# TensorE's order written out by the program: scores, transposes and weighted values between sixths of a step's feed-forward products

## The chip, the cores and the metric

The kernel runs on one core of a Trainium2 chip. TensorE (PE) multiplies matrices into PSUM; VectorE (DVE), ScalarE (ACT) and GpSimd (POOL) do the work by element; SyncE (SP) issues the DMAs. Each engine takes its instructions in the order in which they stand in its own stream. The metric is the device time of one execution in microseconds (us).

## What is computed

Attention that keeps the 32 largest scores of every row, then a gated feed-forward layer on its output:

```
scores = q @ k.T / 8                     # 8 batches x 8 heads, 576 rows, 64 wide
kth    = 32nd largest score of each row
attn   = softmax over the scores >= kth
x      = attn @ v                        # gathered to 4608 tokens x 512
out    = (sigmoid(x @ w_gate) * (x @ w_val)) @ w_out      # 512 -> 1536 -> 512
```

## The kernel before

**Attention.** A step is one pair of heads `p` (4 pairs), one tile `i` of 128 query rows and one batch: 4 full tiles, and a fifth of 64 rows per head that holds both heads (`i == NT`, half the work). A batch goes in two groups of tiles, (0,1,2) and (3,4) in even batches, (0,1) and (2,3,4) in odd ones; inside a group all tiles of a pair come, then the next pair: 160 steps. A step does the following.

- `begin`/`scores`: TensorE writes a head's scores to `pss` (one PSUM buffer of two banks, pool `ps_s`), ACT copies them to `s` (L228). A full tile has two such blocks, here called block 0 and block 1, for its two heads. The products are of split operands: queries `qh`+`ql` (ACT L190, POOL L191), keys likewise (ACT L171, POOL L173).
- `select`: DVE finds the largest of eight segments (`cand`, L286) and from them three rounds of eight (`tops`, `leads`, L290); ACT marks what lies below (`under`, L298, which waits for `leads`); POOL writes `u` (L304, L305); DVE reads the limit `kths` (L312). ACT makes the exponentials `e` (L235), which wait for a small POOL instruction `st` (L294).
- `masked`: DVE multiplies `e` with the mask (L240); POOL spreads the inverse sum to `inv` (L246).
- `turn`: TensorE transposes `e` in three blocks `pt` (two PSUM buffers), ACT copies each to `et` (L328).
- `weigh`, at a pair's last tile of a group: TensorE makes `po` from `et` and the values (L356, L357), DVE scales it to `xf` (L360), ACT and POOL split it into `xh` and `xl` (L363, L364).

**Feed-forward.** A unit is 384 tokens; there are 12. It has three rounds `g`; a round has four gate/value pairs `pz` of 24 products each (L395 to L397) and then four outputs of 12 products each (L414 to L416), all into `ps_f` (three buffers). After a pair come ACT (tanh, L400), DVE (`gf`, L401), ACT (`gh`, L402) and POOL (`gl`, L403), and the outputs read `gh` and `gl` of all four pairs. The weights come from DRAM, split into a high and a low part; the first pass splits them itself, which takes until the third unit's inputs are first allocated (`split_done`).

**Order.** At iteration `n` the program writes: keys and values of step `n+2`, queries of `n+4`, scores of `n+2`, selection of `n`, mask of `n-1`, then as many feed-forward products as a goal allows that follows the rows already turned (`at`) 480 rows behind, then the transposes of `n-2` and, at a group's end, the weighted values. This is a priority only: a scheduler lays out all instructions on a simulated timeline and puts on each engine what is ready there first. So TensorE's stream is not the order of the program. The weighted values have a raised priority and go from the last tile to the first.

Of the kernel before, what the change touches and what calls it, by code (L numbers as in the profile page):

```python
# [10 lines left out]
F32 = mybir.dt.float32  # L11
# [18 lines left out]
def tile_topk_attention_then_gated_ffn(  # L30
# [30 lines left out]
    FETCH, ASK, AHEAD = 2, 4, 2  # L61
# [132 lines left out]
    def scores(qs, ks, i, nm):  # L194

        J = 2 if i < NT else 1
        s = bs.tile([P, 2, S], F32, tag="s", name=f"s_{nm}")
        K = D if len(qs) == 1 else P
        if K == D and J == 2:
# [9 lines left out]
            return s  # L209
# [21 lines left out]
        return s  # L231
# [83 lines left out]
    def turn(e, inv, i, et, nm):  # L315

        ef = e.rearrange("p j s -> p (j s)")
        if i < NT:
            for g in range(3):
# [8 lines left out]
                nc.scalar.activation(et[:, 3 * g : 3 * g + m], pt[:, :m], AF.Copy)  # L328
        else:
# [3 lines left out]
            for h in range(2):  # L333
                nc.scalar.activation(et[:, 5 * h : 5 * h + 4, :REM], pt[:, :, h * REM : h * REM + REM], AF.Copy)
            pt = ps_t.tile([P, 4, P], F32, tag="t", name=f"pt_{nm}_1")
# [3 lines left out]
            for h in range(2):  # L339
                d = slice(h * D, h * D + D)  # L340
                nc.scalar.activation(et[d, 4:10:5, :REM], pt[d, h : 3 : 2 - h, h * REM : h * REM + REM], AF.Copy)

    def weigh(ets, vt, pieces, nm):
# [7 lines left out]
        with tc.high_priority():  # L351
            lead = None
            for et, c, n in reversed(spans):
                with tc.issue_after(lead.ins) if lead is not None else ExitStack():
                    for a in reversed(range(5)):
                        last = nc.tensor.matmul(po[D:, c], vt[:, 5 + a], et[:, 4 + a, :n], start=a == 4, stop=a == 0)  # L356
                        nc.tensor.matmul(po[:D, c], vt[:, a], et[:, a, :n], start=a == 4, stop=a == 0)  # L357
                lead = last
# [8 lines left out]
    def ffn(nm0, xs, t0, general):  # L367
# [17 lines left out]
        for g in range(NG):  # L385
            gs = []
            for f in range(FG):
# [3 lines left out]
                pz = []  # L391
                for u in range(2):
# [5 lines left out]
                    pz.append(ps)  # L398
                gf = pools["f2"].tile([P, U], F32, tag="gf", name=f"gf_{nm}")
                nc.scalar.activation(gf, pz[0], AF.Tanh, scale=0.5)  # L400
                nc.vector.scalar_tensor_tensor(gf, gf, 1.0, pz[1], op0=ALU.add, op1=ALU.mult)  # L401
# [3 lines left out]
                yield 6 * NP * U  # L405
            for e in range(NE):
                if e % 2 == 0:
                    wt = load(NF + g * (NE // 2) + e // 2)
                nm = f"{nm0}_{g}_{e}"
                if g == 0:  # L410
                    acc[e] = pools["f4"].tile([P, U], F32, tag="acc", name=f"acc_{nm}")
                ps = ps_f.tile([P, U], F32, tag="f", name=f"po2_{nm}")
                for f, (gh, gl) in enumerate(gs):
                    nc.tensor.matmul(ps, wt[:, e % 2, 0, f], gh, start=f == 0, stop=False)  # L414
                    nc.tensor.matmul(ps, wt[:, e % 2, 0, f], gl, start=False, stop=False)  # L415
                    nc.tensor.matmul(ps, wt[:, e % 2, 1, f], gh, start=False, stop=f == FG - 1)  # L416
                if g == 0:
                    nc.scalar.activation(acc[e], ps, AF.Copy, scale=0.5)  # L418
                else:
                    part = pools["f2"].tile([P, U], F32, tag="gf", name=f"part_{nm}")  # L420
# [4 lines left out]
                yield 3 * FG * U  # L425

    def run(general):
# [4 lines left out]
        def fetch(m):  # L432
            if m < len(steps) and steps[m][2] == groups[steps[m][0]][1]:
# [4 lines left out]
                values[g, p] = load_values(b, p, f"{mark}{g}_{p}")  # L438

        def begin(m):  # L440
            if m < len(steps):
                g, p, i = steps[m]
                staged[m] = scores(qs.pop(m), keys[groups[g][0], p], i, f"{mark}{groups[g][0]}_{i}_{p}")
# [6 lines left out]
        for m in range(max(FETCH, ASK)):  # L450
            if m < FETCH:
                fetch(m)
            if m < ASK:
                ask(m)
        for m in range(AHEAD):
            begin(m)
# [138 lines left out]
```

## Time and profile before

| what | value |
|---|---|
| runs (3) | 1634.15, 1638.8, 1639.49 us; median 1638.8 |
| profiled execution | 1635.55 us, span 1633.7 us |
| PE busy | 1551.6 us, 95% of the span |
| DVE, POOL, ACT busy | 1262.6, 1178.9, 1159.4 us (77%, 72%, 71%) |
| DMA | 330 MB, 58% of 16 engines' time on the main queue |

Busy time of PE is the union of its instructions' spans; neighbours overlap, so start-to-start distances tell its pace. "Idle before" names the engine whose semaphore ended a wait.

### The profile page before, as it was taken

Reading aid. Unit: us, or ns where it says so; the run is one execution under the profiler, and the core shown is the slowest. Engines: PE = TensorE matmul, PEld = TensorE weight load, DVE = VectorE, ACT = ScalarE, POOL = GpSimd, SP = SyncE. Lnnn points to the kernel's source line nnn. Section 1 sums busy time; section 2 is a strip of 40 time slices with the busy share of each in tenths; the row PEclk is TensorE's granted clock in tenths of the full one; section 3 lists DMA queues with packets and bytes.
Section 4 is the critical chain, followed back from the end, with each engine's and each line's share of the span. In section 5 each row is a group of like instructions: output and inputs, shape, how many; then the busy total and the mean of one; then the engine's idle time right before and its main releaser. Section 6 shows DMA issues by size and latency. Waiting matters only on the chain. (4 is left out here: it accounts for less than half of the span.)

```text
span 1633.7 us, 35681 instructions
## 1 busy us (share of the span) xinstructions
PE 1551.6 (95%) x11378; PEld 1431.1 (88%) x11378; DVE 1262.6 (77%) x5764; ACT 1159.4 (71%) x2551; POOL 1178.9 (72%) x1907
## 2 busy tenths in 40 slices
PE   5878999999999999999999999989999999999998
PEld 2435797889999899999999999979999989999998
DVE  5999779988788788888788868888878778887400
ACT  6888678878676777778776677777767677776421
POOL 4677878888767787788867786787875797775513
PEclk8878999999999999999999999999999999999999
DMA  8546655755555565556555575555555565554575
GB/s 249 184 163 222 257 174 181 253 196 208 201 202 182 186 235 189 202 192 219 205 208 193 177 251 183 192 194 198 201 198 187 203 221 193 188 195 164 184 270 181
DMA packets 88998, 330.03 MB, mean 202 GB/s; under 512 B 9952, under 2 KB 36576, under 8 KB 61920
## 3 DMA queue, kind: packets, MB, share of 16 engines
q1 hardware_dynamic: 88800, 327.65, 58.0%
q8 instruction: 92, 1.51, 0.4%
q14 instruction: 106, 0.87, 0.2%
HBM read 299.30 MB, written 28.31 MB: 201 GB/s over the span
## 5 line engine op out<-in xcount | busy, mean ns | idle before, releaser
L304 POOL TENSOR_TENSOR u<-s,under 128x288 f32<-128x288 f32 x576 | 423.9, 758 | 116.8 <-ACT under L298 109.8
L286 DVE MAX8 cand<-s 128x8 f32<-128x72 f32 x2304 | 346.3, 217 | 107.5 <-ACT s L228 96.6
L395 PE MATMUL pz<-xh,w 128*128 128x384 f32 x1120 | 382.3, 343 | 1.4 <-ACT xh L363 1.1
L396 PE MATMUL pz<-xl,w 128*128 128x384 f32 x1120 | 380.4, 340 | 2.0 <-POOL xl L364 2.0
L397 PE MATMUL pz<-xh,w 128*128 128x384 f32 x1120 | 380.3, 340 | 0.0
L240 DVE SCALAR_TENSOR_TENSOR e<-s,kths,e 128x576 f32<-128x576 f32 x288 | 289.3, 1010 | 3.2 <-ACT e L235 2.9
L312 DVE MAX8 kths<-u 128x8 f32<-128x584 f32 x288 | 219.4, 762 | 89.1 <-POOL u L305 87.0
L235 ACT ACTIVATE e<-s,st 128x576 f32<-128x576 f32 x288 | 210.2, 773 | 103.9 <-POOL st L294 103.4
L298 ACT ACTIVATE under<-s,leads 128x576 fp8e4<-128x576 f32 x288 | 223.0, 775 | 58.0 <-DVE leads L290 54.7
L403 POOL TENSOR_TENSOR gl<-gf,gh 128x384 fp32r<-128x384 f32 x144 | 151.1, 1050 | 100.2 <-ACT gh L402 97.0
L395 PEld LDWEIGHTS pz<-xh,w 128*128 128x128 f32 x1120 | 210.6, 188 | 3.7 <-ACT xh L363 1.8
L396 PEld LDWEIGHTS pz<-xl,w 128*128 128x128 f32 x1120 | 211.2, 189 | 3.0 <-POOL xl L364 2.9
L397 PEld LDWEIGHTS pz<-xh,w 128*128 128x128 f32 x1120 | 210.9, 188 | 0.3
L328 ACT ACTIVATE et<-pt 128x384 f32<-128x384 f32 (+1 forms) x384 | 193.6, 522 | 22.6 <-PE pt L323 12.3
L323 PE MATMUL pt<-ident,e 128*128 128x128 f32 x1152 | 187.6, 282 | 16.5 <-DVE e L240 13.5
L228 ACT ACTIVATE s<-pss 128x576 f32<-128x576 f32 x256 | 164.8, 644 | 40.5 <-PE pss L221 40.0
L415 PE MATMUL po<-gl,w 128*128 128x384 f32 x560 | 190.0, 340 | 1.0 <-POOL gl L403 1.0
L414 PE MATMUL po<-gh,w 128*128 128x384 f32 x560 | 188.0, 346 | 1.3 <-ACT acc L418 1.2
L416 PE MATMUL po<-gh,w 128*128 128x384 f32 x560 | 188.5, 339 | 0.0
L221 PE MATMUL pss<-k,qh 128*128 128x288 f32 (+2 forms) x588 | 168.5, 304 | 15.2 <-ACT s L228 15.1
L323 PEld LDWEIGHTS pt<-ident,e 128*128 128x128 f32 x1152 | 143.3, 144 | 44.8 <-DVE e L240 12.7
L356 PE MATMUL po<-et,v 128*64 128x128 f32 (+1 forms) x1600 | 178.7, 265 | 0.2 <-ACT et L328 0.2
(97 smaller groups left out, 3344.0 us busy)
## 6 DMA issues: line engine op xcount, KB each, us to landing
w<-ws SPq DMA_DIRECT2D x210, 1024.0 KB, 4.9
v<-in_v_dram SPq DMA_DIRECT2D x64, 320.0 KB, 3.1
wraw<-in_w_dram SPq DMA_DIRECT2D x36, 512.0 KB, 4.4
ws<-wsplit SPq DMA_DIRECT2D x36, 512.0 KB, 3.6
qraw<-in_q_dram SPq DMA_DIRECT2D x140, 128.0 KB, 2.3
kraw<-in_k_dram SPq DMA_DIRECT2D x56, 288.0 KB, 3.2
out_dram<-acc SPq DMA_DIRECT2D x48, 192.0 KB, 3.5
q<-in_q_dram SPq DMA_DIRECT2D x20, 128.0 KB, 3.3
```

What stands on the lines that cost most here:

```text
L235: nc.scalar.activation(e[:, j], s[:, j], AF.Exp, bias=st[:, j : j + 1], scale=1.0 / SHRINK)
L240: nc.vector.scalar_tensor_tensor(e[:, j], s[:, j], kth[j], e[:, j], op0=ALU.is_ge, op1=ALU.mult, accum_out=st[:, 4 + j : 5 + j])
L286: nc.vector.max(cand[:, j, 8 * g : 8 * g + 8], s[:, j, g * SEG : (g + 1) * SEG])
L298: nc.scalar.activation(under[:, j], s[:, j], AF.Sign, bias=bound, scale=-CUT, accum_out=sums[:, j : j + 1], saturate=False)
L304: nc.gpsimd.tensor_tensor(u[:, j, c], s[:, j, c], under[:, j, c], op=ALU.mult)
L312: nc.vector.max(kths[:, at[j] : at[j] + 8], u[:, j])
L323: nc.tensor.transpose(pt[:, c], ef[:, k0 : k0 + P], ident)
L328: nc.scalar.activation(et[:, 3 * g : 3 * g + m], pt[:, :m], AF.Copy)
L395: nc.tensor.matmul(ps, wt[:, u, 0, d], xh, start=d == 0, stop=False)
L396: nc.tensor.matmul(ps, wt[:, u, 0, d], xl, start=False, stop=False)
L397: nc.tensor.matmul(ps, wt[:, u, 1, d], xh, start=False, stop=d == NP - 1)
L415: nc.tensor.matmul(ps, wt[:, e % 2, 0, f], gl, start=False, stop=False)
```

## The change

From the iteration in which the weights are split and the third unit's inputs exist, TensorE's stream is put under a manual schedule: its instructions stand as the program writes them, and the scheduler orders the other engines alone. The step is cut up for that. `scores` and `turn` give up control after each block; `ffn` does so after every three products; `weigh` goes forward, without raised priority, one iteration later (`n-3`). In each iteration six pieces are written, each followed by a sixth of the step's feed-forward products: score block 0, transposes, weighted values, transposes, score block 1, transposes. In a round's outputs the first two outputs take the fourth pair's `gh`/`gl` last. The tanh of a pair is written before the value products. Keys are fetched 4 steps ahead instead of 2, values in the step itself instead of 2 ahead. Before the region starts, the scheduler still orders TensorE.

```diff
-    FETCH, ASK, AHEAD = 2, 4, 2
+    KEYS, ASK, AHEAD = 4, 4, 2
...
     def weigh(ets, vt, pieces, nm):
...
-        with tc.high_priority():
-            lead = None
-            for et, c, n in reversed(spans):
-                with tc.issue_after(lead.ins) if lead is not None else ExitStack():
-                    for a in reversed(range(5)):
...
+        for et, c, n in spans:
+            for a in range(5):
...
                     for d, (xh, xl) in enumerate(xs):
                         nc.tensor.matmul(ps, wt[:, u, 0, d], xh, start=d == 0, stop=False)
                         nc.tensor.matmul(ps, wt[:, u, 0, d], xl, start=False, stop=False)
                         nc.tensor.matmul(ps, wt[:, u, 1, d], xh, start=False, stop=d == NP - 1)
+                        if d < NP - 1:
+                            yield 3 * U
+                    if u == 0:
+                        nc.scalar.activation(gf, ps, AF.Tanh, scale=0.5)
+                        yield 3 * U
...
+            for e0 in range(0, NE, 2):
+                wt = load(NF + g * (NE // 2) + e0 // 2)
+                late = FG - 1 if e0 == 0 else FG
+                for e in (e0, e0 + 1):
+                    outs[e] = ps_f.tile([P, U], F32, tag="f", name=f"po2_{nm0}_{g}_{e}")
+                    for f in range(late):
+                        products(e, f)
+                        if f < FG - 1:
+                            yield 3 * U
+                    if late == FG:
+                        collect(e)
+                        yield 3 * U
+                if late < FG:
+                    for e in (e0, e0 + 1):
+                        products(e, late)
+                        collect(e)
+                        yield 3 * U
...
+        for n in range(len(steps) + 3):
+            if not general and region is None and len(bxs) == 2:
+                region = tc.manual_schedule(engines={mybir.EngineType.PE})
+                region.__enter__()
...
+            fetch_values(n)
+            fetch_keys(n + KEYS)
+            ask(n + ASK)
+            goal = max(at - BEHIND, min((at - U) * 1.5, U)) * per_row
+            first, second = begin(n + AHEAD), turned(n - 2) if 2 <= n < len(steps) + 2 else iter(())
+            if region is None:
...
+            else:
+                choose(n)
+                chunks = [first, second, None, second, first, second]
+                begun = work
+                for t, chunk in enumerate(chunks):
+                    if chunk is not None:
+                        next(chunk, None)
+                    elif 3 <= n:
+                        weighed(n - 3)
+                    more(begun + (goal - begun) * (t + 1) / len(chunks))
```

`choose` is the selection of `n` and the mask of `n-1`; `turned` calls `turn`; `weighed` calls `weigh` and appends finished units.

**First place: a score block and its successor.** On TensorE before, in the sixth batch, pair 1: the second block of tile 2, then the first block of tile 3 (`pss` tile_pair_block).

```order
L221 MATMUL pss_2_1_1_15808<-k_1_3_14449,qh_2_1_15486 128x288
L221 MATMUL pss_2_1_1_15808<-k_1_3_14449,ql_2_1_15487 128x288
L221 MATMUL pss_2_1_1_15808<-k_1_3_14449,qh_2_1_15486 128x288
L221 MATMUL pss_2_1_1_15808<-k_1_3_14449,ql_2_1_15487 128x288
L323 MATMUL pt_2_0_1_16078<-ident,e_2_0_15659 128x128 x3
L323 MATMUL pt_2_0_2_16083<-ident,e_2_0_15659 128x128 x3
L326 MATMUL pt_2_0_2_16083<-ident,inv_2_0_15863 128x128
L221 MATMUL pss_3_1_0_15955<-k_1_2_14443,qh_3_1_15638 128x288
L221 MATMUL pss_3_1_0_15955<-k_1_2_14443,ql_3_1_15639 128x288
L221 MATMUL pss_3_1_0_15955<-k_1_2_14443,qh_3_1_15638 128x288
L221 MATMUL pss_3_1_0_15955<-k_1_2_14443,ql_3_1_15639 128x288
```

On TensorE after the change, at the same place, from the end of the six products that follow the second block of tile 2 to the start of tile 3's first block.

```order
L410 MATMUL po_6_2_1_15877<-gh_2_3_15756,w_16_15865 128x384
L411 MATMUL po_6_2_1_15877<-gl_2_3_15757,w_16_15865 128x384
L412 MATMUL po_6_2_1_15877<-gh_2_3_15756,w_16_15865 128x384
L323 MATMUL pt_1_3_2_15912<-ident,e_1_3_15485 128x128 x3
L326 MATMUL pt_1_3_2_15912<-ident,inv_1_3_15675 128x128
L410 MATMUL po_6_2_2_15920<-gh_2_0_15439,w_17_15918 128x384
L411 MATMUL po_6_2_2_15920<-gl_2_0_15440,w_17_15918 128x384
L412 MATMUL po_6_2_2_15920<-gh_2_0_15439,w_17_15918 128x384
L410 MATMUL po_6_2_2_15920<-gh_2_1_15556,w_17_15918 128x384
L411 MATMUL po_6_2_2_15920<-gl_2_1_15557,w_17_15918 128x384
L412 MATMUL po_6_2_2_15920<-gh_2_1_15556,w_17_15918 128x384
L221 MATMUL pss_3_1_0_15968<-k_1_2_14149,qh_3_1_15622 128x288
```

Where seven transposes stood alone between the two blocks, twelve products and four transposes stand.

**Second place: the last `gl` of a round.** On TensorE before, in unit 5's first round, up to the first product that reads the fourth pair's low part `gl_0_3` (the last gate/value product stands 29 products, 10 transposes and 8 score products ahead of it).

```order
L416 MATMUL po_5_0_2_12773<-gh_0_0_12156,w_13_12770 128x384
L414 MATMUL po_5_0_2_12773<-gh_0_1_12319,w_13_12770 128x384
L415 MATMUL po_5_0_2_12773<-gl_0_1_12320,w_13_12770 128x384
L416 MATMUL po_5_0_2_12773<-gh_0_1_12319,w_13_12770 128x384
L414 MATMUL po_5_0_2_12773<-gh_0_2_12441,w_13_12770 128x384
L415 MATMUL po_5_0_2_12773<-gl_0_2_12442,w_13_12770 128x384
L416 MATMUL po_5_0_2_12773<-gh_0_2_12441,w_13_12770 128x384
L221 MATMUL pss_1_2_0_12254<-k_2_4_12036,qh_1_2_11913 128x288
L221 MATMUL pss_1_2_0_12254<-k_2_4_12036,ql_1_2_11914 128x288
L221 MATMUL pss_1_2_0_12254<-k_2_4_12036,qh_1_2_11913 128x288
L221 MATMUL pss_1_2_0_12254<-k_2_4_12036,ql_1_2_11914 128x288
L415 MATMUL po_5_0_0_12613<-gl_0_3_12477,w_12_12610 128x384
```

On TensorE after the change, the same product of the same unit and round.

```order
L410 MATMUL po_5_0_1_12622<-gh_0_1_12290,w_12_12610 128x384
L411 MATMUL po_5_0_1_12622<-gl_0_1_12291,w_12_12610 128x384
L412 MATMUL po_5_0_1_12622<-gh_0_1_12290,w_12_12610 128x384
L410 MATMUL po_5_0_1_12622<-gh_0_2_12383,w_12_12610 128x384
L411 MATMUL po_5_0_1_12622<-gl_0_2_12384,w_12_12610 128x384
L412 MATMUL po_5_0_1_12622<-gh_0_2_12383,w_12_12610 128x384
L221 MATMUL pss_0_3_1_12637<-k_3_7_12205,qh_0_3_12211 128x288
L221 MATMUL pss_0_3_1_12637<-k_3_7_12205,ql_0_3_12212 128x288
L221 MATMUL pss_0_3_1_12637<-k_3_7_12205,qh_0_3_12211 128x288
L221 MATMUL pss_0_3_1_12637<-k_3_7_12205,ql_0_3_12212 128x288
L410 MATMUL po_5_0_0_12612<-gh_0_3_12495,w_12_12610 128x384
L411 MATMUL po_5_0_0_12612<-gl_0_3_12496,w_12_12610 128x384
```

The third output has moved behind the reading of `gl_0_3`; the last gate/value product stands 19 products, 6 transposes and 4 score products ahead of it.

## Rows read from the trace of the kernel before

**Rows 1.** The page's busy times: engine, us, share, instructions.
```profile
PE 1551.6 (95%) x11378; PEld 1431.1 (88%) x11378; DVE 1262.6 (77%) x5764; ACT 1159.4 (71%) x2551; POOL 1178.9 (72%) x1907
```

**Rows 2.** Busy time by stretch: us, length, each engine, clock, DMA share, GB/s.
```profile
100.00:200.00 100.00, 84.93 (x543) 59.94 (x543) 91.33 (x385) 77.07 (x159) 79.18 (x124) 0.90 0.66 235
...
290.00:1530.00 1240.00, 1215.37 (x9390) 1167.92 (x9389) 1005.86 (x4697) 907.62 (x2032) 943.07 (x1544) 0.99 0.58 200
```

**Rows 3.** Waits from 290 to 1530 us: who for whom, total, times, longest.
```profile
ACT e L235 <- POOL st L294: 100.2, 70, 5.0
...
ACT under L298 <- DVE leads L290: 48.5, 52, 4.8
...
PE pss L221 <- ACT s L228: 15.1, 11, 3.2
```

**Rows 4.** TensorE from 1072 us on: start, us, instruction [idle before <-who].
```profile
1072.90 0.30 PE L221 MATMUL pss<-k,ql 128*128 128x288 f32 x1
1073.03 0.82 PE L323 MATMUL pt<-ident,e 128*128 128x128 f32 x6
1074.32 0.33 PE L326 MATMUL pt<-ident,inv 128*128 128x128 f32 x1 [0.47 <-POOL inv L246]
1077.86 0.61 PE L221 MATMUL pss<-k,qh 128*128 128x288 f32 x1 [3.21 <-ACT s L228]
```

**Rows 5.** ScalarE in the same stretch.
```profile
1073.34 2.11 ACT L235 ACTIVATE e<-s,st 128x576 f32<-128x576 f32 x3 [2.68 <-POOL st L294]
1075.35 0.76 ACT L298 ACTIVATE under<-s,leads 128x576 fp8e4<-128x576 f32 x1
1076.02 0.19 ACT L298 ACTIVATION_READ_ACCUMULATOR under<-s,leads 128x1 f32 x1
1076.11 0.40 ACT L190 ACTIVATE qh<-qraw 128x256 fp32r<-128x256 f32 x1
...
1077.18 0.63 ACT L228 ACTIVATE s<-pss 128x576 f32<-128x576 f32 x1
```

**Rows 6.** GpSimd just before.
```profile
1068.10 2.06 POOL L173 TENSOR_TENSOR k<-kraw,k 64x288 fp32r<-64x288 f32 x2
...
1071.45 1.55 POOL L173 TENSOR_TENSOR k<-kraw,k 64x288 fp32r<-64x288 f32 x2
1073.09 0.22 POOL L294 TENSOR_SCALAR st<-tops 128x2 f32<-128x2 f32 x1
```

**Rows 7.** Stretches with a lower clock, columns as in rows 2.
```profile
900.00:940.00 40.00, 37.34 (x267) 36.02 (x266) 32.04 (x156) 26.53 (x59) 29.58 (x49) 0.96 0.55 182
...
1076.00:1090.00 14.00, 11.85 (x61) 11.13 (x62) 13.18 (x71) 11.81 (x29) 11.16 (x21) 0.76 0.31 102
```

**Rows 8.** All engines from 801 us on: products, transposes, the way to `gl`.
```profile
801.20 0.34 PE L396 MATMUL pz<-xl,w 128*128 128x384 f32 x1
...
801.37 0.34 PE L397 MATMUL pz<-xh,w 128*128 128x384 f32 x1
...
802.25 0.49 PE L323 MATMUL pt<-ident,e 128*128 128x128 f32 x3
...
802.75 0.33 PE L416 MATMUL po<-gh,w 128*128 128x384 f32 x1
...
803.40 0.53 DVE L401 SCALAR_TENSOR_TENSOR gf<-gf,pz 128x384 f32<-128x384 f32 x1
...
803.85 1.38 POOL L304 TENSOR_TENSOR u<-s,under 128x288 f32<-128x288 f32 x2 [1.21 <-ACT under L298]
...
803.97 0.52 ACT L402 ACTIVATE gh<-gf 128x384 fp32r<-128x384 f32 x1 [0.20 <-DVE gf L401]
...
805.35 1.02 POOL L403 TENSOR_TENSOR gl<-gf,gh 128x384 fp32r<-128x384 f32 x1
```

**Rows 9.** 1148 to 1242 us, all engines; then ScalarE's L298 alone.
```profile
1148.00:1242.00 94.00, 92.72 (x744) 89.94 (x743) 77.79 (x359) 67.10 (x153) 68.40 (x114) 1.00 0.58 201
...
1148.00:1242.00 94.00, 15.60 (x36) 1.00 0.58 201
```

More of the change, by code (lines that the diff above doesn't have):

```diff
@@ L437, in fetch, with fetch_values @@
                     keys[b, p] = load_keys(b, p, f"{mark}{g}_{p}")
[L438 removed]
+        def fetch_values(m):
+            if m < len(steps) and steps[m][2] == groups[steps[m][0]][1]:
+                g, p, _ = steps[m]
+                values[g, p] = load_values(groups[g][0], p, f"{mark}{g}_{p}")
         def begin(m):
@@ L483, in run, with more @@
                 done[n - 1] = next(parts.pop(n - 1))
-            goal = max(at - BEHIND, min((at - U) * 1.5, U)) * 3 * (2 * NF * NP + NE * NF)
-            while todo and work < goal:
+        def more(upto):
+            nonlocal work
+            while todo and work < upto:
                 cost = next(todo[0], None)
@@ L503, in run @@
-            if i == end - 1:
-                t, left, pieces = b * S + first * P, sum(n for _, n in ets), []
-                while left:
-                    u, c = t // U, t % U
-                    if (u, p) not in xs:
-                        if u % 3 == 2 and len(bxs) == 1:
-                            for _ in todo.pop(0) if todo else ():
-                                pass
-                            split_done()
-                        xs[u, p] = [bxs[u % 3 // 2].tile([P, U], F32R, tag=k, name=f"{k}{mark}_{u}_{p}") for k in ("xh", "xl")]
-                    k = min(left, U - c, 2 * P)
-                    pieces.append((xs[u, p], c, k))
-                    t, left = t + k, left - k
-                weigh(ets, values[g, p], pieces, nm)
@@ L519, in run, with weighed @@
-            at += (P if i < NT else REM) / NP
-            if p == NP - 1 and i == end - 1:
+                ets[g, p] = []
+            et = b4.tile([P, 10, P], F32, tag="et", name=f"et_{mark}{b}_{i}_{p}")
+            e, inv = done.pop(m)
+            ets[g, p].append((et, P if i < NT else REM))
+            yield from turn(e, inv, i, et, f"{mark}{b}_{i}_{p}")
+        def weighed(m):
+            nonlocal unit
+            g, p, i = steps[m]
+            b, first, end = groups[g]
+            if i < end - 1 or (g, p) not in ets:
+                return
+            t, left, pieces = b * S + first * P, sum(n for _, n in ets[g, p]), []
+            while left:
+                u, c = t // U, t % U
+                if (u, p) not in xs:
+                    if u % 3 == 2 and len(bxs) == 1:
+                        for _ in todo.pop(0) if todo else ():
+                            pass
+                        split_done()
+                    xs[u, p] = [bxs[u % 3 // 2].tile([P, U], F32R, tag=k, name=f"{k}{mark}_{u}_{p}") for k in ("xh", "xl")]
+                k = min(left, U - c, 2 * P)
+                pieces.append((xs[u, p], c, k))
+                t, left = t + k, left - k
+            weigh(ets.pop((g, p)), values[g, p], pieces, f"{mark}{b}_{i}_{p}")
+            if p == NP - 1:
@@ L526, in run @@
                 pass
+        if region is not None:
+            region.__exit__(None, None, None)
     run(False)
```

120 lines of the change are left out of this document (62 added, 58 removed).

## The prediction

> **What bounds the kernel now.** I read the page's busy times first: TensorE is busy for 1551.6 of 1633.7 us, DVE for 1262.6 [rows 1]. The windows then show that the stages differ. From 290 to 1530 us TensorE is busy 1215.37 of 1240 us, DVE 1005.86 (81%): TensorE sets the time and stands idle for 24.6 us. From 100 to 200 us it is DVE, with 91.33 of 100 [rows 2]. After 1530 us only feed-forward products are left, and the change alters little there.
>
> So the most that a better TensorE order can give back in the long stage is its idle time and what its clock loses. The list of waits says who causes the idle time: 15.1 us in 11 waits are a score block's first product that waits for ACT's copy `s` [rows 3]; the other 9.5 us have other causes. Other engines wait far more (ACT's `e` 100.2 us for POOL's `st`, ACT's `under` 48.5 us for DVE's `leads`), but their waits cost only what reaches TensorE.
>
> The longest such wait shows how one comes about. A score block ends at about 1073.1; seven transposes follow, and the next block starts only at 1077.86, after 3.21 us of waiting [rows 4]. ACT had been held 2.68 us at `e`, then did two `under` (0.76 + 0.19), `qh` (0.40) and a further `under` before the copy of 0.63 us [rows 5]. It waited for POOL's `st`, 0.22 us long, which stood behind two pairs of key splits (2.06 and 1.55 us) [rows 6]. [...]
>
> **The change, part by part.** *Work.* TensorE has the same 11,378 matmuls. Its paces, start to start: a product 0.17 us (801.20 to 801.37 [rows 8]), a score product 0.13 us (1072.90 to 1073.03 [rows 4]), a transpose 0.11 us (802.25 to 802.75 is three transposes and one product: 0.50 − 0.17 = 3 × 0.11 [rows 8]). That interval also prices the changes of kind, of which the new order has about a quarter more (1274 for 1012 by the order): transposes to product and back show no extra time. I take 0; 260 × 0.01 = 3 us is the other bound, since 0.01 us is as fine as the rows go.
>
> *Idle time that goes.* Products now stand between any two pieces of attention. Counted by those paces, a `pt` buffer is written again after at least 3.0 us (0.9 before), and weighted values follow their last transpose by at least 5.1 us (0 before). Transposes follow their scores by at least 24 us (11 before), so a late `e` reaches TensorE less often. Of the 24.6 us I let 20 go; the 5 kept are small waits that no order removes. Bounds: 24.6 and 0. Of the clock's loss, 40 × 0.04 + 14 × 0.24 = 5 us in the two stretches of [rows 7], I let 4 go; bounds 5 and 0.
>
> *Score copies: +2 us.* `pss` has one buffer, so block 0 of the next step waits until block 1 is copied. By the order, in 99 places of the region this distance is now only 1.48 us (26), 2.08 (19) or 2.52 (54), on average 2.16: one piece with its transposes and six to twelve products. Before, its median was 4.3, but the rest reached down to 0.44. Lower bound 0.69 us, an unhindered copy (0.63 us [rows 5] and some latency): then nothing waits. Upper bound: ACT has an `under` pair, `qh` and the copy to do, 0.76 + 0.19 + 0.40 + 0.63 = 1.98 us [rows 5], and waits for `leads` on the way, 48.5 / 52 = 0.93 us [rows 3]: 2.9 us, 0.75 over the distance, at 99 places 74 us. I take a value near the lower end, 2 us: the order puts such an `under` and `qh` ahead of the copy in 24 places now (55 before), more often a mere `et` copy and `qh`. Behind a score block that waits, every later TensorE instruction waits too; that is the price of an order that is fixed.
>
> *Last `gl` of a round: +4 us.* The third output now comes after the products that read `gl` of the fourth pair. In the second place of the order, 19 products, 6 transposes and 4 score products lie in front: 3.2 + 0.7 + 0.5 = 4.4 us, where there were 7.1. In the trace the way from the last product's end (801.37 + 0.34 = 801.71) over `gf`, `gh` to the end of `gl` (805.35 + 1.02 = 806.37) takes 4.7 us, of which 1.38 us is a `u` pair ahead of it on POOL [rows 8]. Of 33 such places in the region 4 stand at 3.3 us, 4 at 4.1, 15 near 4.5, 10 above 7. By this one way: 4 × 1.4 + 4 × 0.6 + 15 × 0.15 = 10 us. Lower bound 0, since the tanh now comes before the value products, and POOL need not have `u` ahead (4.7 − 1.4 = 3.3). Upper bound: another `u` pair ahead, 23 × 1.4 = 32 us. I take 4, near the lower end.
>
> *Even pace: +8 us.* The goal is the same, but each step now carries 36 or 18 products (6.2 or 3.1 us) instead of what the scheduler pulled forward. In three places of eight steps each, right after a group that ends an odd batch, the new order gives TensorE about 9.05 us a step with its small losses. DVE needs 77.79 us for nine full steps (36 rows of `under`, four a step): 8.64 us each [rows 9]. At DVE's highest share, 0.913 [rows 2], a step takes 9.46 us: (9.46 − 9.05) × 24 = 10 us. Bounds 0 (DVE quite full) and 15; I take 8.
>
> *Other moves.* Keys come two steps sooner: the same DMAs on SP's queue and the same splits on ACT and POOL, in other places; SP's queue has work for 58% of the time (DMA share [rows 2]), and keys wait in memory for their step either way. 0, with POOL's share (943.07 of 1240 [rows 2]) as cover. If a split of 2.06 us lands ahead of `st` as in [rows 6], it costs what the old case cost, 3 us each. Values move two steps later, past the keys' DMAs; `weigh` that reads them is three steps later, some 3 × 8.64 = 26 us: 0. Ahead of the region, DVE sets the pace: 0, ±5 us.
>
> [...] From 100 to 200 us, with many transposes and few products, the granted clock is 0.90 [rows 2]. [...]
>
> **Sum.** The profiled execution took 1635.55 us: 1635.55 − 20 − 4 + 0 + 2 + 4 + 8 + 0 = 1625.6. The median of the runs, 1638.8, is 3.2 above that execution, so 1629 us in the terms of the median, 0.6% less.
>
> **Rivals.** *Full gain.* All idle time and lower-clock time goes and nothing comes: 1638.8 − 24.6 − 5 = 1609 us. For it: the distances above all grew, and most waits are rare events. Against it: two distances shrank.
>
> *No change.* Waits on ACT and POOL (100.2 and 48.5 us [rows 3]) are no shorter, and TensorE meets them elsewhere, with as much idle time as now: 1635 to 1642. That the order is not what the change says is excluded for TensorE, since both excerpts show it; it can fail to matter, though, if the simulated order already sat as well as the 95% busy share [rows 1] allows.
>
> *Slower by score copies.* The mechanism of the 2.9 us above: the copy of block 1 stands behind an `under` that waits for `leads`. It decides as soon as the copies end on average more than the 2.16 us after the block. If it does so in a third of the 99 places, 33 × 0.75 = 25 us, and half of the old idle time stays (8 us more): 1629 + 25 − 2 + 8 = 1660. For it: the old case of [rows 4 and 5] has exactly this order on ACT. Against it: fewer such places now.
>
> *Slower by `gl`.* POOL has two `u` pairs ahead of `gl` in each of the 23 close places: 1629 + 32 − 4 = 1657. For it: POOL waits for `under` in its own order (1.21 us at 803.85 [rows 8]), with `gl` behind. Against it: the tanh is earlier.
>
> **How the numbers follow.** Forecast 0.40 (its own range 1614 to 1638), full gain 0.14, no change 0.14, slower by copies 0.20, slower by `gl` 0.12. The likeliest gives 1629; two in ten may lie outside 1605 to 1661, which reaches past the full gain on one side and takes in the slower cases' middle on the other. A measurement of this kernel can tell 0.3%, some 5 us, from no change. Below 1634 lie the full gain and nearly nine tenths of the forecast: 0.50; within 5 us of 1638.8 the no-change case and the rest of the forecast: 0.18; the two slower cases: 0.32.
>
> **What would show it.** Right: TensorE's idle time from 290 to 1530 us falls to some 5 to 15 us, the row for `pss` on `s` falls below 15.1, and no stretch like 1076 to 1090 with a clock of 0.76 is left. Each of the two slower cases has its row among the waits: TensorE's `pss` for `s` with many more than 11 waits, or its outputs' product for POOL's `gl`. The even pace shows as waits of `pss` or `pt` after full steps in which DVE is above 0.9 busy. The forecast is wrong if TensorE's idle time is as large as before, or if the time goes to the first 290 us.

## The result and the profile after

The changed kernel takes 1651.3 us (4 runs, 1650.08 to 1652.53); the kernel before takes 1637.13 (4 runs: the three earlier ones and one beside the changed kernel). The ratio is 1.0088 (95% interval 1.0066 to 1.0109): slower by 0.9%, where 0.6% faster was forecast. The profiled execution took 1652.19 us, its span 1650.4.

The page's busy times hardly differ from [rows 1]:

```profile
PE 1555.4 (94%) x11378; PEld 1428.8 (87%) x11378; DVE 1241.3 (75%) x5764; ACT 1174.1 (71%) x2551; POOL 1163.7 (71%) x1907
```

The windows say where the time went. First the kernel after, then two windows of the one before (the window from 100 to 200 us stands in [rows 2]); columns as there.

```profile
100.00:200.00 100.00, 81.20 (x419) 51.24 (x420) 88.66 (x364) 79.56 (x166) 84.11 (x127) 0.83 0.63 215
...
320.00:400.00 80.00, 67.61 (x471) 61.88 (x471) 57.28 (x257) 53.59 (x121) 60.52 (x101) 0.94 0.55 185
...
420.00:1530.00 1110.00, 1088.35 (x8456) 1049.19 (x8455) 893.27 (x4255) 824.30 (x1821) 823.21 (x1381) 1.00 0.58 199
```

```profile
320.00:400.00 80.00, 76.17 (x595) 73.20 (x595) 66.62 (x317) 61.53 (x139) 67.60 (x113) 1.00 0.58 201
...
420.00:1530.00 1110.00, 1090.09 (x8419) 1050.58 (x8418) 897.57 (x4209) 805.28 (x1804) 833.70 (x1369) 0.99 0.57 198
```

From 100 to 200 us TensorE starts 419 matmuls instead of 543, from 320 to 400 us 471 instead of 595, at lower granted clocks (0.83 instead of 0.90, 0.94 instead of 1.00). From 420 to 1530 us it starts 8456 instead of 8419. So the long stage won a little, and two short stretches at the start lost.

Matmuls differ in length, so a better measure is **work done**: all matmuls started by a time, each at its undisturbed pace (start to start: the paces of the prediction, taken finer, 0.173 us for a product; the first batch's score products, whose operands aren't split, some 0.25 us, weighted values 0.054 us, the weight splits' 0.45 and 0.23 us), added up. It comes to 1458 us in both kernels. By 300 us the changed kernel has done 203.9 us of work (before: 212.6), by 400 us 279.7 (303.0), by 1500 us 1316.8 (1334.7). That is 8.7 us behind, then 23.3, then 17.9: the start costs 23 us and the long stage gives back 5.4.

**The start.** At 160 us the changed kernel is 2.8 us of work ahead, at 220 us 8.4 behind, and that hardly changes until 300. In between the first feed-forward product comes late: it ran at 168.24 us before and now runs at 181.86. It doesn't wait for the inputs that it reads first: those of the unit's first two pairs are weighted by 94 us (before: by 105). Those of the fourth pair are later, too: their `xh` is done at 174.6 us and their `xl` at 182.2 (before: 171.4 and 177.0). On TensorE the first product stands right behind a weight split `wrest`, before:

```profile
166.66 1.17 PE L148 MATMUL wrest<-wraw,ident 128*128 128x512 f32 x2 [0.93 <-DVE wraw L141]
...
168.24 0.42 PE L395 MATMUL pz<-xh,w 128*128 128x384 f32 x1
```

and after:

```profile
180.77 2.07 PE L148 MATMUL wrest<-wraw,ident 128*128 128x512 f32 x2 [0.55 <-DVE wraw L141]
181.86 1.31 PE L394 MATMUL pz<-xh,w 128*128 128x384 f32 x1
```

It is the 24th of 36 splits (two for each of 18 weight tiles). The splits write to the same PSUM buffers, `ps_f`, as the feed-forward, and in all 17 kernels timed here the first product follows this row within 1.6 us. The splits stay late: the last of all is done at 335 us instead of 314. It waits for POOL:

```profile
335.37 0.50 PE L150 MATMUL wrest<-wsplit,plus 128*128 128x512 f32 x1 [1.59 <-POOL wsplit L145]
```

On POOL its part (L145) stands behind a `u` pair, two key splits and `ql`:

```profile
327.89 1.54 POOL L304 TENSOR_TENSOR u<-s,under 128x288 f32<-128x288 f32 x2
329.51 1.57 POOL L173 TENSOR_TENSOR k<-kraw,k 64x288 fp32r<-64x288 f32 x2
331.17 0.73 POOL L191 TENSOR_TENSOR ql<-qraw,qh 128x256 fp32r<-128x256 f32 x1
...
332.27 1.56 POOL L173 TENSOR_TENSOR k<-kraw,k 64x288 fp32r<-64x288 f32 x2
333.91 1.41 POOL L145 TENSOR_TENSOR wsplit<-wsplit,wt_lead 128x256 fp32r<-128x256 f32 x2
```

The written order begins near 281 us, where ACT copies the first score block that it holds. Just behind the last split, TensorE stands idle in it for DVE and ACT (its instructions from 340 us on that wait):

```profile
344.35 0.48 PE L356 MATMUL po<-et,v 128*64 128x128 f32 x1 [3.85 <-DVE xf L359]
...
352.44 0.45 PE L394 MATMUL pz<-xh,w 128*128 128x384 f32 x1 [1.42 <-ACT xh L362]
```

The weighted values wait 3.85 us for `xf` of the pair before; the products written behind them are the ones that read those values, and wait again. The granted clock is 1.00 from 281 to 335 us and 0.50 from 335.9 to 339.3 and from 342.8 to 349.6, around the waits of 1.59 and 3.85 us.

That `xf` is late goes back to the last split. The values that it reads were written by 324.2 us. But `xf` has two buffers, and one is free again only when the third unit's `xh` and `xl` have been made from it; these lie in the memory that the splits use, so they start when the last split is copied. (In run 14 below DVE waits 0.91 us for this `xl` before the same `xf`.)

```profile
335.91 0.60 ACT L151 ACTIVATE wsplit<-wrest 128x512 fp32r<-128x512 f32 x1 [0.24 <-PE wrest L150]
336.40 0.39 ACT L362 ACTIVATE xh<-xf 128x64 fp32r<-128x64 f32 x2
...
342.56 0.59 POOL L363 TENSOR_TENSOR xl<-xf,xh 128x64 fp32r<-128x64 f32 x2
...
343.83 0.46 DVE L359 TENSOR_TENSOR xf<-po,et 128x128 f32<-128x128 f32 x2
```

Before, the same chain ran from 315.80 us (the last copy's end) to 319.42 (`xf`), and TensorE had other work.

**The long stage.** TensorE's waits from 420 to 1530 us, first after, then before:

```profile
PE pss L221 <- ACT s L228: 10.3, 15, 1.3
...
PE po L411 <- POOL gl L404: 9.6, 6, 2.4
...
PE pz L395 <- POOL xl L363: 1.5, 2, 0.8
```

```profile
PE pss L221 <- ACT s L228: 12.1, 9, 3.2
...
PE pt L332 <- ACT et L328: 1.8, 2, 0.9
...
PE pz L396 <- POOL xl L364: 1.7, 2, 1.1
...
PE po L415 <- POOL gl L403: 1.0, 2, 0.5
```

The two lists add up to 21.4 us after and 19.4 before (with four more rows, 2.8 us together). The order took away the small waits and made the one for `gl`, which comes in a period of 369 us; the waits for score copies hardly shrank. So what the long stage won isn't in its waits. It is mostly in the weighted values, which now stand in one block per pair and group: from 420 to 1530 us TensorE changes between them and other matmuls 96 times instead of 142. A change costs some 0.12 us (run 4 below shows it), so 46 fewer give an estimated 5.5 us. One of the waits for `gl` on TensorE, with the round's last gate/value product first, and POOL before it:

```profile
581.30 0.34 PE L396 MATMUL pz<-xh,w 128*128 128x384 f32 x1
...
585.38 0.34 PE L410 MATMUL po<-gh,w 128*128 128x384 f32 x1
588.13 0.44 PE L411 MATMUL po<-gl,w 128*128 128x384 f32 x1 [2.41 <-POOL gl L404]
...
588.95 0.53 PE L411 MATMUL po<-gl,w 128*128 128x384 f32 x1
...
589.91 0.53 PE L411 MATMUL po<-gl,w 128*128 128x384 f32 x1
```

```profile
583.50 1.59 POOL L173 TENSOR_TENSOR k<-kraw,k 64x288 fp32r<-64x288 f32 x2
585.16 1.36 POOL L304 TENSOR_TENSOR u<-s,under 128x288 f32<-128x288 f32 x2
...
587.09 0.99 POOL L404 TENSOR_TENSOR gl<-gf,gh 128x384 fp32r<-128x384 f32 x1
```

A key-split pair and a `u` pair stand ahead of `gl`. After the wait, three products take 589.91 − 588.95 = 0.96 us, 0.32 each instead of 0.17: the granted clock is 0.50 from 588.5 to 591.9 us. Such 3.4 us follow each of the three long waits (the others from 957.1 and 1325.8 us, at 0.51 and 0.50). The score copies are still late in places, by the very chain of the prediction; here ACT before a copy that the next block waits 1.28 us for:

```profile
622.31 0.76 ACT L298 ACTIVATE under<-s,leads 128x576 fp8e4<-128x576 f32 x1
622.98 0.19 ACT L298 ACTIVATION_READ_ACCUMULATOR under<-s,leads 128x1 f32 x1
623.07 0.40 ACT L190 ACTIVATE qh<-qraw 128x256 fp32r<-128x256 f32 x1
623.50 0.65 ACT L228 ACTIVATE s<-pss 128x576 f32<-128x576 f32 x1
```

### The profile page after: what moved, and what is told of

The parts are those of the page before. It is cut to its first block, busy times and chain, and to the rows that moved or that the text cites. A ratio compares the mean times of both kernels' runs of the same rounds, so it can differ in the third digit from the quotient of the medians.

```text
span 1650.4 us, 35802 instructions
## 1 busy us (share of the span) xinstructions
PE 1555.4 (94%) x11378; PEld 1428.8 (87%) x11378; DVE 1241.3 (75%) x5764; ACT 1174.1 (71%) x2551; POOL 1163.7 (71%) x1907
## 4 chain that ended last, share of the span: by engine, by line
PE 73%; POOL 8%; ACT 7%; DVE 6%; issue 3%; DMA 1%; POOLq 0%; ACTq 0%; DVEq 0%; SPq 0%
PE pz L394 11%; PE pz L395 11%; PE pz L396 11%; PE pss L221 8%; PE po L356 7%; PE pt L323 6%; PE po L410 5%; PE po L411 5%; PE po L412 5%; POOL u L304 3%; ACT under L298 2%; DVE e L240 1%; POOL k L173 1%; DVE kths L312 1%; DVE cand L286 1%
## 5 line engine op out<-in xcount | busy, mean ns | idle before, releaser
L304 POOL TENSOR_TENSOR u<-s,under 128x288 f32<-128x288 f32 x576 | 414.6, 742 | 97.2 <-ACT under L298 89.9
L394 PE MATMUL pz<-xh,w 128*128 128x384 f32 x1120 | 403.9, 361 | 1.4 <-ACT xh L362 1.4
L396 PE MATMUL pz<-xh,w 128*128 128x384 f32 x1120 | 377.2, 337 | 0.0
L298 ACT ACTIVATE under<-s,leads 128x576 fp8e4<-128x576 f32 x288 | 222.8, 775 | 89.0 <-DVE leads L290 84.6
L240 DVE SCALAR_TENSOR_TENSOR e<-s,kths,e 128x576 f32<-128x576 f32 x288 | 272.6, 953 | 7.7 <-ACT e L235 7.4
L328 ACT ACTIVATE et<-pt 128x384 f32<-128x384 f32 (+1 forms) x384 | 199.3, 522 | 60.5 <-PE pt L323 56.1
L395 PEld LDWEIGHTS pz<-xl,w 128*128 128x128 f32 x1120 | 212.1, 189 | 3.5 <-POOL xl L363 3.0
L323 PE MATMUL pt<-ident,e 128*128 128x128 f32 x1152 | 195.2, 280 | 9.9 <-DVE e L240 6.1
L410 PE MATMUL po<-gh,w 128*128 128x384 f32 x560 | 203.8, 365 | 0.0
L356 PEld LDWEIGHTS po<-et,v 128*64 128x64 f32 x1600 | 163.4, 140 | 32.8 <-issue 21.2
L412 PE MATMUL po<-gh,w 128*128 128x384 f32 x560 | 190.3, 340 | 0.0
L356 PE MATMUL po<-et,v 128*64 128x128 f32 (+1 forms) x1600 | 183.9, 270 | 3.9 <-DVE xf L359 3.8
L357 PE MATMUL po<-et,v 128*64 128x128 f32 (+1 forms) x1600 | 184.2, 270 | 0.0
L323 PEld LDWEIGHTS pt<-ident,e 128*128 128x128 f32 x1152 | 149.3, 143 | 39.6 <-ACT et L328 8.2
```

What stands on the lines that cost most here:

```text
L240: nc.vector.scalar_tensor_tensor(e[:, j], s[:, j], kth[j], e[:, j], op0=ALU.is_ge, op1=ALU.mult, accum_out=st[:, 4 + j : 5 + j])
L298: nc.scalar.activation(under[:, j], s[:, j], AF.Sign, bias=bound, scale=-CUT, accum_out=sums[:, j : j + 1], saturate=False)
L304: nc.gpsimd.tensor_tensor(u[:, j, c], s[:, j, c], under[:, j, c], op=ALU.mult)
L323: nc.tensor.transpose(pt[:, c], ef[:, k0 : k0 + P], ident)
L394: nc.tensor.matmul(ps, wt[:, u, 0, d], xh, start=d == 0, stop=False)
L395: nc.tensor.matmul(ps, wt[:, u, 0, d], xl, start=False, stop=False)
```

## The experiments

Each was timed against the kernel before on the same chip. "Work" is work done, as above, in us; the last columns are the median and the ratio to before with its interval.

| kernel | first product | last split | work by 300 | 320 to 400 | by 420 | us | ratio |
|---|---|---|---|---|---|---|---|
| before | 168 | 314 | 212.6 | 72.6 | 322.4 | 1637.1 | |
| after | 182 | 335 | 203.9 | 59.5 | 299.1 | 1651.3 | 1.0088 (1.0066 to 1.0109) |
| 1 keys 2 ahead | 172 | 322 | 213.9 | 68.6 | 314.1 | 1639.0 | 1.0011 (1.0001 to 1.0021) |
| 2 order from 40 | 182 | 329 | 205.1 | 66.1 | 307.7 | 1643.1 | 1.0033 (1.0022 to 1.0045) |
| 3 weighted values first | 174 | 317 | 214.2 | 65.9 | 315.5 | 1639.5 | 1.0018 (1.0008 to 1.0027) |
| 4 no written order | 180 | 326 | 207.6 | 66.8 | 310.2 | 1663.0 | 1.0158 (1.0141 to 1.0175) |
| 5 = 1 + 2 + 3 | 175 | 320 | 210.7 | 65.2 | 311.3 | 1641.7 | 1.0040 (1.0027 to 1.0053) |
| 6 = 5 + third output | 176 | 322 | 208.7 | 63.0 | 308.4 | 1630.0 | 0.9957 (0.9943 to 0.9971) |
| 7 = 6 + even pieces | 173 | 318 | 212.1 | 66.0 | 313.1 | 1617.3 | 0.9888 (0.9871 to 0.9904) |
| 8 = 4 + weighted values first | 175 | 315 | 213.7 | 70.0 | 319.3 | 1645.6 | 1.0054 (1.0037 to 1.0071) |
| 9 splits first | 166 | 317 | 218.3 | 60.9 | 311.4 | 1637.6 | 1.0004 (0.9994 to 1.0014) |
| 10 = 7 + 9 | 158 | 319 | 213.4 | 70.6 | 319.8 | 1608.1 | 0.9824 (0.9805 to 0.9843) |
| 11 after + third output, even pieces | 180 | 333 | 206.7 | 59.5 | 302.3 | 1628.1 | 0.9954 (0.9938 to 0.9970) |
| 12 = 11 + 3 | 173 | 320 | 215.3 | 63.4 | 312.4 | 1616.1 | 0.9884 (0.9853 to 0.9915) |
| 13 = 9 + 2 | 165 | 310 | 220.2 | 72.8 | 327.8 | 1622.4 | 0.9913 (0.9894 to 0.9933) |
| 14 before + splits first | 165 | 317 | 215.0 | 72.0 | 320.9 | 1635.4 | 0.9984 (0.9974 to 0.9993) |
| 15 = 13 + third output, even pieces | 165 | 310 | 220.2 | 73.1 | 327.9 | 1599.9 | 0.9768 (0.9744 to 0.9791) |

**1. Keys 2 ahead.**

```diff
-    KEYS, ASK, AHEAD = 4, 4, 2
+    KEYS, ASK, AHEAD = 2, 4, 2
```

> The changed kernel, with keys fetched 2 steps ahead again instead of 4; nothing else. Comparing the two traces by TensorE work done at a given time, the changed kernel loses some 11 us between 160 and 220 us and some 13 us between 320 and 400 us, and wins 5 us later. Theory: the first loss comes from key splits that stand earlier on ACT and POOL, ahead of the last weight splits, so that the first feed-forward product starts at 182 us instead of 168. Then the first product comes near 168 to 172 us again and the time falls by about 9, to 1642 us. Rival (the weighted values without raised priority are late, and with them the feed-forward's inputs): the first product stays near 182 us, the time near 1651 us.

1639.0 us, 12 less, and the first product at 172: as the theory said, and 3 us more.

**2. Written order from iteration 40.**

```diff
-            if not general and region is None and len(bxs) == 2:
+            if not general and region is None and len(bxs) == 2 and n >= 40:
```

> The changed kernel, with TensorE's written order starting at iteration 40 (the third batch) instead of 24; nothing else. Theory: the second loss is the written order's beginning, where the weight splits are not done and TensorE waits in order for DVE and POOL. Then the loss from 320 to 400 us goes, the time falls by about 12, to 1639 us, and the first loss stays. Rival (a fixed order costs as much wherever it begins, or the loss is the late feed-forward's): a loss of the same size appears at the new beginning, the time stays near 1651 us.

1643.1 us, 8 less; 66.1 us of work from 320 to 400 instead of 59.5, half of the way to 72.6. The first loss stayed. No loss of that size shows at the new beginning, near 428 us (work by 420 is 8.6 us more than in the changed kernel, by 500 7.8 more).

**3. Weighted values in priority, last tile first, until the written order begins** (the removed lines of `weigh`, under the condition that no written order has begun).

> The changed kernel, with the weighted values in raised priority and from the last tile to the first, as before, as long as the written order hasn't begun; nothing else. Theory (key splits): the first product stays near 182 us, the time near 1651 us. Rival (the weighted values are late): the first product comes near 168 us, and the time falls by about 10, to 1641 us.

1639.5 us: the time is the rival's. But 1 has the same effect without this edit, so neither is the cause alone. In both, the fourth pair's inputs come sooner, too (`xl` done at 168.1 us here and 165.2 in 1, 182.2 in the changed kernel), so 3 doesn't tell late inputs from late splits.

**4. No written order** (`if n < 0` in the line of 2).

> The changed kernel without the written order: the scheduler orders TensorE to the end, all other edits stay (keys 4 ahead, values later, weighted values forward without priority, products given out by threes, the late pair of the first two outputs). Theory: the loss from 320 to 400 us goes (12 us), the first loss stays, and the 5 us won later are lost: about 1644 us. Rival (the written order is what costs, all along): 1638 us or less, as before.

1663.0 us, slower than either: both theories missed. From 420 to 1530 us its page has TensorE busy without a gap, and yet fewer matmuls started (8312) than in the others:

```profile
420.00:1530.00 1110.00, 1110.00 (x8312) 1033.42 (x8311) 905.61 (x4180) 813.74 (x1791) 821.51 (x1357) 1.00 0.56 196
```

The weighted values (L356, L357) are what takes longer. The groups by line of this kernel, then of the changed one:

```profile
L357 PE MATMUL po<-et,v 128*64 128x128 f32 (+1 forms) x1600 | 219.2, 275 | 0.0
L356 PE MATMUL po<-et,v 128*64 128x128 f32 (+1 forms) x1600 | 218.7, 275 | 0.3 <-ACT et L328 0.3
```

```profile
L357 PE MATMUL po<-et,v 128*64 128x128 f32 (+1 forms) x1600 | 184.2, 270 | 0.0
L356 PE MATMUL po<-et,v 128*64 128x128 f32 (+1 forms) x1600 | 183.9, 270 | 3.9 <-DVE xf L359 3.8
```

As long each (275 and 270 ns), but the union of their spans is 35 us larger: without priority the scheduler scatters them. Between two kinds of matmuls with the weighted values on one side the start-to-start distance is 0.09 to 0.15 us above the pace, 0.12 on average. From 420 to 1530 us this trace has 394 such changes of kind (the 287 of the next expectation leave some kinds out), the changed kernel 96, the one before 142.

**8. No written order, weighted values in priority all along**, to test that.

> The changed kernel without the written order, with the weighted values in priority and from the last tile to the first all along, as before. Without the written order and without that priority it took 1663 us, with 287 changes of kind into or out of the weighted values at 0.1 to 0.15 us each and no long wait. Theory (the scheduler without priority scatters the weighted values among other work, and each change costs): 1637 to 1641 us. Rival (keys 4 ahead, values in the step, products by threes or the late pair cost it): above 1650 us.

1645.6 us: of the 26 us that 4 lost against the kernel before, 17 are back; the time lies between theory and rival. But 9.1 us of it are there by 420 us, at the start. In the long stage the changes of kind fall from 394 to 142, an estimated 30 us, and only 4.2 us more work by 1500 us comes of it, for TensorE, which hadn't waited at all in 4, waits again, at a granted clock of 0.99 where it was 1.00:

```profile
420.00:1530.00 1110.00, 1086.59 (x8325) 1046.81 (x8324) 886.73 (x4167) 800.71 (x1793) 823.55 (x1352) 0.99 0.57 197
```

So each change costs TensorE time, but most of that time is lost to waits where the changes are gone. What keeps the time 5 us above the theory isn't shown.

**5. Edits 1, 2 and 3 together.**

> The changed kernel with the three edits of the first experiments together: keys 2 steps ahead, weighted values in priority until the written order begins, written order from iteration 40. Theory (two losses at the start that add up: some 11 us by 220 us, some 8 of the 13 us from 320 to 400 us by the early beginning): the first edit or the second alone gave 12 us, either takes the first loss away and both together no more; the third adds 8: 1651 - 12 - 8 = 1631 us, faster than before. Rival (one loss, which any of the three takes away): 1639 us.

1641.7 us: the theory of two losses, as it stood, fell. The last split is at 320 us (322 and 317 with 1 or 3 alone), but the work by 300 is 210.7 (213.9 and 214.2). What the scheduler makes of these edits doesn't add up.

**6. The third output ahead of the last `gl`.**

```diff
-            for e0 in range(0, NE, 2):
...
+            for e, f in [(0, 0), (0, 1), (0, 2), (1, 0), (1, 1), (1, 2), (2, 0), (2, 1),
+                         (0, 3), (2, 2), (1, 3), (2, 3), (3, 0), (3, 1), (3, 2), (3, 3)]:
+                if f == 0:
+                    begin_output(e)
+                products(e, f)
+                if f == FG - 1:
+                    collect(e)
+                yield 3 * U
```

> The kernel of the run before in this list, with two products groups of the third output in front of the fourth pair's last products: the reader of the last gl stands six products (1.04 us) later. Theory (the three waits of 2.4 us and the three near 0.9 us for gl between 420 and 1530 us cost 10.6 us, with the half clock after them 5 us more): the waits fall to 1.5 and 0 us, no half clock follows them, 8 to 10 us less than the run before. Rival (the wait moves: the fourth output needs the first one's PSUM buffer earlier, or another wait comes later): 2 us less or nothing.

11.7 us less than 5. The waits from 420 to 1530 us:

```profile
PE pss L221 <- ACT s L228: 12.4, 17, 1.6
...
PE po L415 <- POOL gl L408: 4.4, 3, 1.5
```

5.2 us less waiting for `gl`, each long wait 1 us shorter. The lower clock behind the long waits (in the changed kernel three stretches of 3.4 us at 0.50) is worth 5.1 us more if all of it is gone, an estimate: 10.3 us. (The profiled executions differ by 7.3 us only: that of 6 was the slowest of its six, and has 2.9 us less work by 420.)

**7. Block 1 in the fourth piece.**

```diff
-                chunks = [first, second, None, second, first, second]
+                chunks = [first, second, None, first, second, second]
```

> The kernel of the run before in this list, with score block 1 in the fourth piece of a step instead of the fifth, so that three sixths of a step's products stand on each side of a block. Theory (the waits of a score block's first product for ACT's copy, 11 to 13 us from 420 to 1530 us, come from the distance of only two sixths between block 1 and the next block 0): they fall below 4 us, 8 us less than the run before. Rival (ACT copies late because of what stands ahead on ACT, whatever the distance): same time, the waits move to block 1 of the same step or to the transposes.

12.7 us less than 6 (in the profiled executions 4.7 us of work more is there by 420, and 13.0 comes behind). The waits for score copies are gone, though nothing ahead of the copies on ACT was taken away:

```profile
PE po L415 <- POOL gl L408: 3.9, 3, 1.3
...
PE po L414 <- ACT part L425: 3.4, 3, 1.1
```

The second row is new: an output's first product waits for ACT to collect an earlier one, as the rival of 6 had it.

**9. Weight splits in priority.**

```diff
     def split_weight(idx, held):
+        with tc.high_priority():
...
```

> The changed kernel with the weight splits in raised priority on all engines; nothing else. Over the runs so far, TensorE's work done by 420 us falls with the time at which the last weight split is done: 322 us of work at 314 us before, 299 at 335 in the changed kernel, 308 to 319 at 315 to 329 in the others, about 1 us of work for 1 us. Theory (the late splits set the loss at the start): the last split is done by 315 us, the work by 420 us is near 320, the time falls by 15 to 20, to 1631 to 1636 us. Rival (both only go with how far attention has come, which DVE sets): splits early, attention late, work by 420 us and time as in the changed kernel, within 5 us of 1651.

1637.6 us, 13.7 less, a little short of the theory: the last split is at 317 us and the work by 420 is 311.4. The work by 300 us is 14 us more; but from 320 to 400 us the kernel loses as much as the changed one. Its window, with granted clock 0.91 and DVE less busy than before, and two of TensorE's waits in it:

```profile
320.00:400.00 80.00, 69.70 (x515) 66.55 (x513) 55.16 (x259) 51.29 (x115) 56.37 (x100) 0.91 0.50 172
```

```profile
326.64 0.32 PE L352 MATMUL po<-et,v 128*64 128x128 f32 x1 [3.30 <-DVE xf L355]
...
336.06 0.69 PE L390 MATMUL pz<-xh,w 128*128 128x384 f32 x1 [3.65 <-ACT xh L358]
```

These are the waits of the changed kernel at 344 and 352 us, behind the same chain: here the last split's copy ends at 318.63 us and `xf` starts at 326.12. Splits that end sooner don't spare TensorE the wait; it comes to the weighted values sooner, too.

**13. Splits in priority, written order from 40**, all other parts of the change kept.

> The changed kernel with the weight splits in raised priority and the written order from iteration 40. With the priority alone TensorE had 218 us of work done by 300 us (204 in the changed kernel, 213 before) but only 60.9 us more from 320 to 400 us (59.5 in the changed kernel, 72.6 before, 70.6 in the 1608 us kernel, whose order begins at 40). Theory (two causes at the start: late splits up to 300 us, the order's early beginning from 320 to 400): 66 to 70 us from 320 to 400, 8 us less, 1630 us. Rival (having run ahead by 300 us only fills buffers that DVE empties; what is won is given back by 400 us whatever the order): 61 us from 320 to 400, 1638 us.

1622.4 us, better than the theory: 29 us less than the changed kernel, 15 less than 9. The same window:

```profile
320.00:400.00 80.00, 79.78 (x607) 73.98 (x603) 68.67 (x327) 61.37 (x138) 71.29 (x119) 1.00 0.59 202
```

TensorE with almost no gap (0.7 us of waiting for `xf`), and DVE, ACT and POOL busier too. The rival (DVE's pace) is refuted.

**14. The kernel before with splits in priority**, as a control.

> The kernel before with the weight splits in raised priority; nothing else. Theory (the change delayed the splits, which before were in time): nothing to win, 1633 to 1639 us. Rival (splits in priority help any order): 10 us less, 1626 us.

1635.4 us, 0.16% less: as good as nothing, and the last split no sooner (317 us). The priority makes good what the change had lost.

**11 and 12. The long stage's two edits on the changed kernel's own start, and on that of 3.**

> The changed kernel with the two edits of the long stage alone (third output ahead of the last gl, block 1 in the fourth piece); its start as it was. Theory (the two edits act from 420 us on and add to any start: 12 and 12.5 us in the runs before): 1651 - 24 = 1627 us. Rival (they also needed the later beginning of the written order): above 1635 us.

> As the run before in this list, with the weighted values in priority until the written order begins, keys 4 ahead, written order from iteration 24. Theory (additive): 1639.5 - 24 = 1615 us. Rival: 1622 us or more.

1628.1 and 1616.1 us, 23 us less than each one's base: they add to these starts as to that of 5.

**10 and 15. All that helped.**

> The fastest kernel so far (the three edits of the start, the third output ahead of the last gl, block 1 in the fourth piece: 1617 us, last split at 318 us, 313 us of work by 420) with the weight splits in raised priority. Theory: last split by 312 us, 320 us of work by 420, 1610 us. Rival: 1617 us.

> The kernel of 1622 us (weight splits in priority, written order from iteration 40) with the two edits of the long stage: third output ahead of the last gl, block 1 in the fourth piece. Theory (start and long stage add up): 1622 - 24 = 1598 us. Rival (with TensorE that full another engine sets the pace, DVE in the stretches of three full tiles): 1605 us or more.

1608.1 and 1599.9 us, both times as the theories said. But in 10 the last split isn't sooner (319 us where 312 was forecast), and yet the work by 420 is the forecast 319.8: the last split isn't what orders the starts. The first product comes at 158 there. Run 15 is the fastest, 2.3% below the kernel before.

## Why the prediction was wrong

**The step that failed** is the last of "Other moves": "Ahead of the region, DVE sets the pace: 0, ±5 us", with the 0 for the keys beside it; for the region's beginning the sum has no term. Measured: 8.7 us of work lost by 300 us, most of it ahead of the region, and 14.6 more by 400, inside it. Two causes, told apart by 9, 13 and 14. First, the edits that weren't meant for the start (keys earlier, weighted values without priority) change the scheduler's layout there, and the weight splits come late; put first, they give back 13.7 us, and give nothing to the kernel before. That it is the splits' lateness, and not something else in the layout that the priority moves, is argued from the first product, which stands right behind a split in every kernel. Second, the written order begins at iteration 24, while splits still run: at the end of the chain from the last split over `xh`, `xl` and `xf` TensorE waits in order, and the products written behind wait for the same values. In 9 the chain comes sooner, and TensorE waits for it all the same (60.9 us of work from 320 to 400). Beginning at 40, with the scheduler still ordering TensorE when the last split comes, gives 15 us more.

The prediction looked at DVE's 91% in the start and took it for what sets the pace there. From 320 to 400 us DVE is busy 57.28 of 80 us (66.62 before): when TensorE waits, DVE has less to do too. Why keys and priority delay the splits only together (1 and 3 each restore most, 5 less) stays open; the trace shows key splits ahead of one on POOL, no more. From 281 to 420 us the granted clock was 0.50 for 10.2 us, around the waits of 1.59 and 3.85 us, and 1.00 for the rest.

**Idle time that goes: −20, and −4 for the clock.** The small waits went, as said. But the sum is 21.4 us after against 19.4 before (420 to 1530 us), since score copies and `gl` wait instead. The stretches at clock 0.50 are 10.2 us in all there, instead of 13.6: −1.7 us.

**Last `gl`: +4.** The waits are 9.6 us (before: 1.0), and 10.2 us at clock 0.50 lie behind them, 5.1 us of loss, which no term held. The 10 us of "this one way", before it was taken down to 4, came near by luck: it was 23 places at up to 1.4 us, and it is six, three of them at 2.41. The distance had been worked out rightly: 585.72 − 581.30 = 4.4 us without the wait. But it counts from the last product's start and the way of 4.7 us from its end, 0.3 us later; and the way was 588.08 − 581.64 = 6.4 us, since POOL had a `u` pair and a key-split pair ahead of `gl`.

**Score copies: +2.** This term was too small: 10.3 us in 15 waits where 2, and a part of the 5 us kept, was forecast, within its bounds of 0 and 74. The mechanism is there on ACT. That it is the distance, 7 showed.

**Even pace: +8.** In the first of its three places, and alike in the others, TensorE stands idle for 0.81 us, for ACT's copies, and DVE is busy 64.27 of 74 us, not above 0.9. That is 2.4 us in all.

```profile
420.00:494.00 74.00, 73.19 (x584) 70.60 (x583) 64.27 (x321) 56.59 (x126) 58.20 (x95) 1.00 0.57 199
```

**Changes of kind: 0** is right for products and transposes (from 625.37 to 625.87 us of the changed kernel three transposes and a product take 0.50 us, 3 × 0.11 + 0.17). For the weighted values it is 0.09 to 0.15 us each (4), and there the new order saves some 5.5 us by having fewer of them, which the prediction did not look for.

So the sign was wrong by the start alone; the long stage won 5.4 us where the sum had 10, and by another way. With the start mended and all else as changed (13) the kernel takes 1622.4 us, where 1629 was forecast. Some 5 us of that is a start better than before (327.8 us of work by 420, 322.4 before), so with the old start it would be near 1628, an estimate. That this meets the forecast is luck: the idle time did not fall. Neither of the slower rivals is what happened.

## What to carry to other kernels

An order written out by hand can pay where every engine runs in a steady rhythm; begin it only after the prologue is over (of the two beginnings tried here the later was 8 and 15 us better), since within it the engine waits in line for whatever else is late (3.85 us for `xf` here). An edit to priorities or prefetch distances moves the prologue as well, so follow the work done over time from zero on, not the busy share of the long stage. In a fixed order, count the distance from each producer to its reader and spread the work so that the shortest distance covers the worst queue ahead of the producer: two edits of a few lines gave 23 us.

## What had not been expected

The kernel with TensorE 100% busy from 420 to 1530 us (1110.00 of 1110) was the slowest of all, at 1663 us. Some 12 of its 26 us lie in the start. In the long stage weighted values scattered among other matmuls cost 0.09 to 0.15 us at each change, which the profile shows as busy time. And a wait of 2.4 us can cost more than itself: in the changed kernel 3.4 us at a granted clock of 0.50, a loss of 1.7 us, followed each of three.
